# Two layers of linear attention and gated MLP on one core: Strassen for half of K's pairs, a third two-level product in one down stage, and a new order at the start and at the hand-overs

## The chip, the cores and the metric

One Trainium2 chip, one core of it. The metric is the device time of one execution in microseconds; the runs shown are three of the same kernel. A profiled execution gives the trace; its span runs from the first to the last instruction.

Engines in the text: PE (TensorE, matmul), ACT (ScalarE), DVE (VectorE), POOL (GpSimd), SP (SyncE, which issues all DMA here).

## The reference

Sequence 2048, width 1024, 32 heads of 32, MLP width 3584, bf16. The block is applied twice with the same weights:

```python
def _A_ref(x, wqkv, wo):                       # linear attention
    q, k, v = split(x @ wqkv)
    phi = lambda t: where(t > 0, t + 1, exp(t)) + 1e-6
    pq, pk = phi(q), phi(k)
    kv = einsum("bhsd,bhse->bhde", pk, v);  z = einsum("bhsd->bhd", pk)
    o = einsum("bhqd,bhde->bhqe", pq, kv) / (einsum("bhqd,bhd->bhq", pq, z)[..., None] + 1e-6)
    return merge_heads(o) @ wo
def _B_ref(x, w_gate, w_up, w_down):           # gated MLP, no activation
    return ((x @ w_gate) * (x @ w_up)) @ w_down
for _ in range(2):
    x = x + _A_ref(_layernorm(x), A_wqkv, A_wo)
    x = x + _B_ref(_layernorm(x), B_w_gate, B_w_up, B_w_down)
```

## The kernel before

**A program with one order for each engine.** The kernel appends operations to `P.add(engine, ...)` in one hand-chosen order. Each engine runs its own operations in that order; waits are derived from what an operation reads and writes in SBUF pages and PSUM banks, and become semaphores. So the order in which the Python calls are made is the schedule, and an operation late on one engine holds all that is behind it there. All DMAs are issued by SP, in order too. The 16 tiles of 128 rows stay in SBUF (`x_res`); the normalized, transposed input of a stage is `xnT`.

**Layer A** (`layer_A`). In layer one, the projections are plain: `proj_kh` and `proj_qh` do 8 matmuls of 128x512 for one tile and one half of the columns. Layer norm of the next tiles (`LN.start`: statistics; `b_one`: normalize; `step_t`: transpose) is woven between. K goes two tiles ahead of Q (`NHOLD = 2`). For each half, ACT takes the exponential out of PSUM (`ex`) and DVE finishes phi from PSUM and the exponential (`fin`); POOL adds up z (`z_add`). While this goes on, `pt_ops` makes sums of Q's weight blocks (`ptq`, one piece per tile from the fifth) and stores them to `pt_scratch` for layer two.

In layer two, `kq_pairs` does two tiles at a time. K is `plain`: four steps of 8 matmuls a pair. Q is `strassen`: seven steps of 4 matmuls, `st1, st5, st6, st2, st7, st3, st4`, with the transformed weights `T` from `pt_scratch` and sums of the input blocks made by `s_sums`. In a Strassen pair, `st1` and `st5` are followed by ACT copies out of PSUM, and `st6` and `st7` by a DVE `join` that adds a saved product into another bank; the next accumulation into the bank read waits for it. Steps are placed on a line by position (`at(pos, ...)`, with `QLAG`, `QEND`, `LNP`, `SPOS`, `SSTEP`) and run sorted by it: K's and Q's steps alternate, with layer norm steps (`flow_step`) and reloads of the normalized rows (`xr_load`) between. `SEP` says for which of K and Q phi is finished by halves (`fin1`) instead of by whole tiles (`fin2`). K uses PSUM banks 0 to 3, Q 4 to 7, and four buffers hold exponentials (`ebuf`).

Both layers then form `xr^T pk` in chunks (`gchunk`, L1291), multiply by the value weights (`kvt`), normalize queries (`norm`), and multiply by the folded output weights (`y_grp`, 8 matmuls for one tile and one half, L1383). The first steps of the gate/up stage, the list `pro`, can be run early, one PE operation at a time, by `pro_step`.

**Layer B** (`layer_B`). Two passes of 1024 rows. `gateup` works on pairs of column units with Strassen's seven products (L1470), some of them split once more (two-level, L1540). `down` multiplies the hidden activations, held as four blocks `hA` to `hD`, by the down weights, again with seven products, named by digits, in the order `DPROD[ps_]`. A one-level product is 4 row tiles x 14 matmuls of 128x512 (L2020); a two-level one (`two_level`) is 7 steps x 2 x 7 matmuls of 128x256 (L1918), with operand sums from `a_sums`. Weights come through a ring of five slots (`ring_issue`). `d_two` says which products are two-level:

```python
DPROD = ["1274653", "1674253"]

def d_two(first, ps_):
    return "532" if ps_ else "" if first else "53"
```

The second pass (`ps_ = 1`) uses the chained form (`chain_step`): products "1", "6", "7" and "4" accumulate in the same four PSUM banks, DVE takes out each intermediate sum, and the operand for the next product is formed by DVE tile by tile. The first pass uses separate banks and its own sequence. During it, `x_pop` makes the operand sums for the second pass's gate/up, and `stash` and `sp_load` move rows and weight sums.

Layer one's first pass is told apart as `jit`: it makes the gate/up weight sums itself.

**The start.** SP issues row tile 0, K's first weight half, tile 1, K's second half, tile 2, Q's first half, tile 3, Q's second half, and the other tiles. PE starts tile 0 after its normalize and transpose.

Of the kernel before, what the change touches and what calls it, by code (L numbers as in the profile page):

```python
# [180 lines left out]
def build_kernel(nc, A_x, A_wqkv, A_wo, B_w_gate, B_w_up, B_w_down, out):  # L181
    _, S, D = A_x.shape
# [13 lines left out]
    KSTR = False  # L196
    QLAG = 0.284
    QEND = 0.102
    SEP = "q"
    LNP = (0.474, 0.5)  # L200
    SPOS = 0.283
    SSTEP = 0.14
    CUP = 9
    KP0 = 1
# [124 lines left out]
    with ExitStack() as es:  # L329
# [36 lines left out]
        O_RT = [[O_R + i * 2048 for i in range(8)], [RB + SZ_HB + i * 2048 for i in range(9)] + [RE + i * 2048 for i in range(3)]]  # L366
# [93 lines left out]
        def ln_a(i, act=False, oj=0):  # L460
# [9 lines left out]
            for h in range(2):  # L470
                P.add("dve", (lambda h: lambda e: e.bn_stats(st[j][:, 6 * h:6 * h + 6], x_res[:, i, (D // 2) * h:(D // 2) * (h + 1)]))(h),
                      rd=r_x(i, (D // 2) * h, (D // 2) * (h + 1)), wr=R(O_ST[j] + 24 * h, 24))
# [35 lines left out]
        class LN:  # L508
# [26 lines left out]
            def start(self, i):  # L535
                assert i == self.n
                act = self.stat_act
                j = ln_a(self.order[i], act, self.o_junk)
# [174 lines left out]
        DPROD = ["1274653", "1674253"]  # L713

        def d_two(first, ps_):
            return "532" if ps_ else "" if first else "53"

        def d_units(first, ps_):
            r = []
            for q in DPROD[ps_]:  # L720
# [121 lines left out]
        def x_ops(pair, prods, jit=False):  # L842
            t1, t2, t3, t4 = t_ops(pair)
            tp = {q: tp_ops(pair, q, jit) for q in "1325"}
            has = lambda q: [(q, f) for f in tp[q]] if q in prods else []
            return [("t1", t1)] + has("1") + [("t2", t2), ("t3", t3)] + has("3") + [("t4", t4)] + has("2") + has("5")
# [90 lines left out]
        def layer_A(lnp, nxt, first, pro):  # L937
# [11 lines left out]
            def proj(w, rw, i):  # L949
                bank = B_KQ[kq_i[0] % len(B_KQ)]  # L950
                kq_i[0] += 1

                def fn(e):
                    return [e.matmul(psb(bank), xnT[:, k, i * 128:(i + 1) * 128], w[:, k, :],  # L954
                                     start=(k == 0), stop=(k == KT - 1)) for k in range(KT)]
# [12 lines left out]
            def proj_kh(i, h):  # L968
                proj(wkh[first][h], R(O_WKH[first][h], 8192), i)
# [27 lines left out]
            def kq_pairs():  # L997
                BG = {"k": [0, 1, 2, 3], "q": [4, 5, 6, 7]}
                ROLE = [dict(a=0, d=1, b=2, c=3), dict(a=0, b=1, d=2, c=3)]
                OP5 = {"k": RC, "q": RC + 2048 if KSTR else RC + 2 * SZ_SLOT + 4096}  # L1000
# [3 lines left out]
                def at(pos, fn):  # L1004
                    ev.append((pos, len(ev), fn))
# [4 lines left out]
                def bk(kind, p):  # L1010
                    r = ROLE[0 if kind == "k" and (p < KP0 or not KSTR) else p % 2]
# [6 lines left out]

                def ebuf():
                    r = e_cnt[0] % 4  # L1020
                    e_cnt[0] += 1
                    return O_E[r]
# [30 lines left out]
                def plain(kind, p):  # L1053
# [4 lines left out]
                    def step(i, h, bank, last, other):  # L1058
                        if h == 0:
                            eb[i] = ebuf()  # L1060
# [1185 lines left out]
```

## Time and profile before

| | |
|---|---|
| median of three runs | 1447.18 us |
| runs | 1447.4, 1445.64, 1447.18 us |
| profiled execution, its own time | 1446.97 us |
| its span | 1445.2 us |
| granted TensorE clock | full speed |
| HBM read, written | 237.24 MB, 62.13 MB |
| matmuls | 8294 |
| K/Q matmuls of layer two, plain (L945) and Strassen (L1115) | 288 and 196 |
| down matmuls, one-level (L2020) and two-level (L1918) | 1120 and 784 |

The page gives for each engine the busy time, its share of the span and the number of instructions. The chain of work that ended last is followed back from the last instruction; its shares say which engine set the end. In a group's row, the part behind the first bar is busy time and mean duration of one, and the part behind the second is how long the engine stood idle just before these instructions and what released it. In a timeline row, the first figure is the start, the second the length, and the bracket the idle time before it and its releaser. Stages by time in this trace: layer A of layer one to about 243 us, its MLP to 737, layer A of layer two to 960 (K and Q to 836), its MLP to the end.

### The profile page before, as it was taken

The page shows a single profiled execution, that of the slowest core. Times are in us where ns is not written, and L with a number is a line of the kernel's source. Part 1 is how long each engine was busy: PE and PEld are TensorE (multiplying, and loading weights), DVE is VectorE, ACT ScalarE, POOL GpSimd, SP SyncE. Part 2 cuts the span into 40 slices and gives each one's busy share as a digit, 9 for nine tenths or more (in the row PEclk, how much of TensorE's full clock was granted, in tenths as well). Part 3 has the DMA queues.
Part 4 walks back from the last instruction along what each step waited for, and adds up shares of the span by engine and source line. Part 5 has one row for each costly group of instructions (what it writes and reads, how often), then busy time and mean ns, then how long its engine had stood idle before and what let it go on. Part 6 is the DMA issues. An engine that isn't in the chain of part 4 may idle for free.

```text
span 1445.2 us, 21993 instructions
## 1 busy us (share of the span) xinstructions
PE 1433.9 (99%) x8294; PEld 800.4 (55%) x8294; DVE 1128.6 (78%) x2027; ACT 680.2 (47%) x1438; POOL 227.5 (16%) x260
## 2 busy tenths in 40 slices
PE   8999999999999999999999999999999999999999
PEld 3444444555544555554664444456666457666547
DVE  6766889889867799877677779879877786777856
ACT  3652256677720255550156423567777005777401
POOL 4543733000000000000044346300000000000000
PEclk9999999999999999999999999999999999999999
DMA  6334757987879899986896067679975779887657
GB/s 233 88 79 118 151 125 155 290 298 249 294 288 338 262 271 294 293 257 225 253 341 195 0 173 151 155 213 274 282 260 197 241 247 296 264 264 257 205 164 239
DMA packets 377993, 324.41 MB, mean 224 GB/s; under 512 B 178208, under 2 KB 326048, under 8 KB 377632
## 3 DMA queue, kind: packets, MB, share of 16 engines
q1 hardware_dynamic: 377888, 323.02, 74.5%
q8 instruction: 65, 1.06, 0.3%
q14 instruction: 40, 0.33, 0.1%
HBM read 237.24 MB, written 62.13 MB: 207 GB/s over the span
## 4 chain that ended last, share of the span: by engine, by line
PE 92%; DVE 4%; DMA 2%; ACT 1%; issue 0%; SPq 0%; POOL 0%; DVEq 0%
PE ps L1470 25%; PE ps L1540 17%; PE ps L2020 16%; PE ps L1291 8%; PE ps L954 6%; PE ps L1383 6%; PE ps L1918 6%; PE ps L945 4%; PE ps L1115 3%; DVE arena L821 2%; DVE arena L824 1%; DMA arena<-in_A_wqkv_dram 1%; DMA arena<-in_B_w_up_dram 1%; DMA arena<-in_B_w_down_dram 1%; PE ps L1303 0%
## 5 line engine op out<-in xcount | busy, mean ns | idle before, releaser
L821 DVE TENSOR_TENSOR arena<-arena 128x512 f16<-128x512 f16 (+7 forms) x752 | 414.1, 577 | 75.9 <-ACT arena L1584 47.6
L1470 PE MATMUL ps<-arena 128*128 128x512 f16 x1808 | 446.5, 379 | 0.7 <-ACT ps L1500 0.7
L824 DVE SCALAR_TENSOR_TENSOR arena<-ps,arena 128x512 f16<-128x512 f32 (+2 forms) x448 | 298.8, 686 | 76.0 <-PE ps L2020 52.2
L1540 PE MATMUL ps<-arena 128*128 128x256 f16 x2324 | 311.8, 273 | 1.7 <-DVE ps L1559 1.3
L1540 PEld LDWEIGHTS ps<-arena 128*128 128x128 f16 (+1 forms) x2324 | 226.2, 98 | 105.0 <-DVE ps L1559 5.8
L1470 PEld LDWEIGHTS ps<-arena 128*128 128x128 f16 (+1 forms) x1808 | 176.4, 98 | 141.8 <-ACT ps L1500 1.4
L2020 PE MATMUL ps<-arena 128*128 128x512 f16 (+1 forms) x1120 | 243.2, 379 | 0.0
L2020 PEld LDWEIGHTS ps<-arena 128*128 128x128 f16 x1120 | 109.6, 98 | 131.3
L1475 ACT ACTIVATE arena<-ps 128x512 f16<-128x512 f32 x224 | 134.0, 598 | 94.0 <-PE ps L1470 90.8
L1556 ACT COPY ps<-ps 128x256 f32<-128x256 f32 x220 | 81.1, 369 | 128.5 <-PE ps L1540 121.4
L1559 DVE TENSOR_TENSOR ps<-ps,arena 128x256 f32<-128x256 f32 x220 | 92.3, 428 | 36.5 <-PE ps L1540 18.4
L474 POOL TENSOR_SCALAR arena<-arena 128x1 f32<-128x1 f32 x48 | 19.5, 407 | 626.1 <-DVE arena L473 626.1
L954 PE MATMUL ps<-arena 128*128 128x512 bf16 x512 | 112.5, 379 | 3.8 <-DMA arena<-in_A_wqkv_dram 1.1
L1291 PE MATMUL ps<-arena 128*128 128x512 bf16 x512 | 115.4, 379 | 0.0
L1383 PE MATMUL ps<-arena 128*128 128x512 bf16 x512 | 111.0, 379 | 0.0
L1922 ACT COPY ps<-ps 128x256 f32<-128x256 f32 x32 | 11.4, 357 | 209.2 <-PE ps L1918 147.1
L1214 POOL TENSOR_TENSOR arena<-arena 128x1024 f16<-128x1024 f32 x32 | 79.2, 2476 | 70.2 <-DVE arena L1212 69.0
L1500 ACT COPY ps<-ps 128x512 f32<-128x512 f32 x112 | 64.2, 573 | 52.0 <-PE ps L1540 44.5
L1918 PE MATMUL ps<-arena 128*128 128x256 f16 (+1 forms) x784 | 87.0, 273 | 0.1
L978 POOL TENSOR_TENSOR arena<-arena 128x512 f32<-128x512 f32 x60 | 74.8, 1266 | 74.1 <-DVE arena L1040 44.0
L954 PEld LDWEIGHTS ps<-arena 128*128 128x128 f16 x512 | 49.5, 98 | 63.0 <-DMA arena<-in_A_wqkv_dram 1.6
L1383 PEld LDWEIGHTS ps<-arena 128*128 128x128 f16 x512 | 50.1, 98 | 60.2
(77 smaller groups left out, 1215.6 us busy)
## 6 DMA issues: line engine op xcount, KB each, us to landing
arena<-w_scratch SPq DMA_DIRECT2D x84, 512.0 KB, 4.9
arena<-sp_scratch SPq DMA_DIRECT2D x56, 512.0 KB, 5.8
arena<-t_scratch SPq DMA_DIRECT2D x29, 896.0 KB, 6.8
arena<-in_B_w_down_dram SPq DMA_DIRECT2D x21, 896.0 KB, 6.9
w_scratch<-arena SPq DMA_DIRECT2D x28, 512.0 KB, 6.5
sp_scratch<-arena SPq DMA_DIRECT2D x28, 512.0 KB, 4.1
arena<-in_B_w_gate_dram SPq DMA_DIRECT2D x42, 256.0 KB, 5.0
arena<-in_B_w_up_dram SPq DMA_DIRECT2D x42, 256.0 KB, 3.2
```

Source lines behind the costliest of these rows:

```text
L821: P.add("dve", lambda e: e.tensor_tensor(out=out, in0=a, in1=b, op=op), rd=rd, wr=wr, prd=prd)
L824: P.add("dve", lambda e: e.scalar_tensor_tensor(out=out, in0=a, scalar=sc, in1=b, op0=ALU.mult, op1=op1), rd=rd, wr=wr, prd=prd)
L954: return [e.matmul(psb(bank), xnT[:, k, i * 128:(i + 1) * 128], w[:, k, :], start=(k == 0), stop=(k == KT - 1)) for k in range(KT)]
L1291: return [e.matmul(psb(bank), xr[:, t, j * 128:(j + 1) * 128], pk[:, h, t, :], start=(t == 0), stop=(t == NST - 1)) for t in range(NST)]
L1383: return [e.matmul(psb(bank), xnT[:, g, i * 128:(i + 1) * 128], wp[:, g, dh * 512:(dh + 1) * 512], start=(dh == 0 and g == 0), stop=(g == ...
L1470: P.add("pe", lambda e: [e.matmul(psb(bank), w[:, k, :], x[:, k, :], start=(start and k == 0), stop=(k == 3), skip_group_check=True) for k ...
L1475: P.add("act", lambda e: e.activation(t, psb(bank), AF.Copy, scale=SG), prd=[bank], wr=r)
L1540: P.add("pe", lambda e: [e.matmul(psb(bank)[:, 256 * half:256 * half + 256], w[:, k, :], xx[:, k, :], start=(start and k == 0), stop=(k == ...
L1556: P.add("act", lambda e: e.copy(psb(dst[c])[:, 0:256], lo), prd=[bk], pwr=[dst[c]])
L1559: P.add("dve", lambda e: e.tensor_tensor(out=psb(dst[c])[:, 256:512], in0=lo, in1=c5, op=ALU.add), prd=[bk], rd=rc5, pwr=[dst[c]])
L1918: P.add("pe", lambda e: [e.matmul(psb(bank)[:, 256 * half:256 * half + 256], a[:, k, :], w[:, k, :], start=(start and k == 0), stop=(k == ...
L2020: return [e.matmul(psb(bank), hv[:, 7 * hf + k, t * 128:(t + 1) * 128], w[:, k, :], start=(start and hf == 0 and k == 0), stop=(hf == 1 an ...
```

## The change

- **Loads at the start:** tile 1 goes ahead of K's first weight half, and the other tiles come one place earlier against the weights.
- **Start of layer one's layer A:** the first half of tile 1's statistics goes ahead of tile 0's normalize on DVE; tile 1's transpose goes between the two halves of tile 0's first eight matmuls; K's first column half is done for tiles 0 and 1 before the second. The order of K and Q is the same (K first) throughout.
- **Strassen for K:** `KSTR = True`, `KP0 = 4`: K's pairs 4 to 7 of layer two use `strassen`. Layer one makes sums of K's weight blocks too and stores them (`ptq` gets five more pieces), and layer two loads them at its start; Q's first block of the second column half is loaded at the end of the stage.
- **Order of layer two's K/Q stage:** written out in `KQ_SEQ` in place of the sort by position. Phi is finished one step later (`pend`), by halves for K too (`SEP = "qk"`), with three exponential buffers (`NEB = 3`), because the fourth holds a saved product.
- **Early heads:** the first gate step of layer one (`P1A+`) and up to three steps of layer two's prologue run between the last `y` groups.
- **Layer two's first down stage:** the chained order, and product "2" two-level as well as "5" and "3"; the sums for it lie in the used part of `xnT`, and its intermediate sums in other buffers (`O_RT`), one of them row tile 15's, after it is stashed. `x_pop`, `stash` and one `sp_load` move to other products.

```diff
-    KSTR = False
-    QLAG = 0.284
-    QEND = 0.102
-    SEP = "q"
+    KSTR = True
+    NEB = 3
+    KQ_SEQ = "K00 S00 S01 K01 S02 S03 L K02 K03 K10 L X K11 Q00 K12 Q01 X L ... X Q64 L Q65 Q66 V W O"
+    SEP = "qk"
...
-    KP0 = 1
+    KP0 = 4
...
-        DPROD = ["1274653", "1674253"]
+        DPROD = {(True, 0): "1274653", (True, 1): "1674253", (False, 0): "1674253", (False, 1): "1674253"}
+        DTWO = {(True, 0): "", (True, 1): "532", (False, 0): "532", (False, 1): L2D}
...
+                def fin1(*a):
+                    pend.append(lambda: fin1_(*a))
...
-                for _, _, f in sorted(ev, key=lambda t: t[:2]):
+                for _, _, tk, f in run:
+                    if tk[0] not in "KQ":
+                        f()
+                        continue
+                    if tk[2] == "0":
+                        flush()
+                    n = len(pend)
                     f()
+                    for _ in range(min(n, len(pend))):
+                        pend.pop(0)()
+                flush()
...
             if first:
                 lnp.start(0)
-                lnp.b_one()
-                lnp.start(1)
+                lnp.start(1, lnp.b_one)
...
+                proj_kh(0, 0, b0, range(4))
+                lnp.step_t(1)
+                proj_kh(0, 0, b0, range(4, KT))
+                ev[0][0](0)
+                lnp.b_one()
+                lnp.start(3)
+                proj_kh(1, 0, b2)
+                ev[1][0](0)
+                lnp.step_t(1)
+                for i, b in enumerate((b1, b3)):
+                    proj_kh(i, 1, b)
...
+                if not first and i == NST - 1:
+                    pro_step(pro, 1)
                 y_grp(tok[i], 0, i)
...
+                if i == NST - 2 or not first and i == NST - 1:
+                    pro_step(pro, 1)
...
-                npro = 0 if jit else [tk[:2] in early for _, tk in seq].index(False)
+                npro = [tk[:2] in early for _, tk in seq].index(False)
+                if jit:
+                    npro = 1
+                    seq.insert(0, seq.pop([tk for _, tk in seq].index("P1A+")))
...
-                if ps_:
+                chain = ps_ or not first
+                if chain:
                     hs.update({"7": (hE, RB), "3": (hA, O_HA)})
...
-                if q == "2" and t == 3:
+                if q == ("2" if first else "1") and t == 3:
                     for k in range(5):
                         stash(11 + k)
...
+                elif not first and q in "453":
+                    x_pop({"4": 2, "5": 1 if t > 1 else 0, "3": 3}[q])
...
-                if q == "3" and t == 0 and not first:
+                if q == "3" and t == 2 and not first:
                     sp_load(1, 1, "53")
...
+        xload(1)
         load_w("k", 0)
-        xload(1)
+        xload(2)
         load_w("k", 1)
-        xload(2)
+        xload(3)
         load_w("q", 0)
-        xload(3)
+        xload(4)
+        xload(5)
         load_w("q", 1)
```

220 lines of the change are left out of this document (136 added, 84 removed).

## The prediction

> **What bounds the kernel now.** I read the page first: busy times, then the chain, then the groups.
>
> ```profile
> span 1445.2 us, 21993 instructions
> ...
> PE 1433.9 (99%) x8294; PEld 800.4 (55%) x8294; DVE 1128.6 (78%) x2027; ACT 680.2 (47%) x1438; POOL 227.5 (16%) x260
> ...
> PE 92%; DVE 4%; DMA 2%; ACT 1%; issue 0%; SPq 0%; POOL 0%; DVEq 0%
> ```
>
> TensorE is busy 99% of the span and holds 92% of the chain. What one matmul costs is its spacing in an unbroken run, which the chain in order of time gives (start, length, what).
>
> ```profile
> 61.87 55.41 PE ps L954 x256
> ...
> 1361.75 48.35 PE ps L2020 x224
> 1410.10 32.24 PE ps L1918 x294
> ```
>
> A 512-column matmul costs 55.41/256 = 0.2164 us or 48.35/224 = 0.2158 us, a 256-column one 32.24/294 = 0.1097 us. So a matmul that goes is worth its whole spacing, if the other engines still feed PE. Next the waits of PE (engine, line, releaser: us, times, longest):
>
> ```profile
> PE ps L1540 <- DVE ps L1559: 1.3, 2, 0.7
> PE ps L954 <- DMA arena<-in_A_wqkv_dram: 1.1, 1, 1.1
> PE ps L954 <- ACT arena L598: 1.1, 1, 1.1
> ...
> PE ps L954 <- DVE arena L662: 0.5, 1, 0.5
> PE ps L1115 <- DVE ps L1119: 0.2, 1, 0.2
> ```
>
> PE waits little, and most of it at the start and where layer A hands over to layer B. That is all that better ordering can win; the rest must come from matmuls.
>
> **Part 1: matmuls removed.** Layer two's K projection: pairs 4 to 7 of eight go from `plain` (4 steps of 8) to `strassen` (7 steps of 4), so 4 x (32 - 28) = 16 matmuls of 512 columns go: 16 x 0.2164 = 3.46 us. Layer two's first down stage: product "2" goes from 4 tiles x 14 = 56 matmuls of 512 to 7 x 2 x 7 = 98 of 256: 56 x 0.2158 = 12.08 against 98 x 0.1097 = 10.75, so 1.33 us go. Together 4.8 us.
>
> The Trainium skill speaks against the second: "TensorE: Matmul & The Clock Gate", Back-to-back issue gap, gives a sustained 131 ns at 512 columns and 81 ns at 128. Taken straight between, an estimate from that page, 256 columns cost about 98 ns, and the product would grow by about 2.3 us. The trace has 216 and 110 ns over hundreds of matmuls, and the measurement decides.
>
> **Part 2: the start.** The timeline of the first 20 us, and a piece of the chain (eight transposes):
>
> ```profile
> 5.77 0.55 DVE L504 TENSOR_SCALAR arena<-arena 128x1024 f16<-128x1024 bf16 x1 [1.00 <-POOL arena L476]
> ...
> 7.93 1.90 PE L954 MATMUL ps<-arena 128*128 128x512 bf16 x8 [0.94 <-ACT arena L590]
> ...
> 7.98 1.42 DVE L471 BATCH_NORM_STATS2 arena<-arena 128x6 f32<-128x512 bf16 x2 [1.67 <-DMA arena<-in_A_x_dram]
> ...
> 9.44 0.21 DVE L473 BATCH_NORM_AGGREGATE arena<-arena 128x2 f32<-128x12 f32 x1
> ...
> 10.98 1.90 PE L954 MATMUL ps<-arena 128*128 128x512 bf16 x8 [1.15 <-DMA arena<-in_A_wqkv_dram]
> ...
> 11.71 1.42 DVE L471 BATCH_NORM_STATS2 arena<-arena 128x6 f32<-128x512 bf16 x2 [0.51 <-DMA arena<-in_A_x_dram]
> ...
> 13.41 1.01 ACT L598 COPY arena<-ps 128x1024 f16<-128x1024 f16 x1
> ...
> 14.47 3.63 PE L954 MATMUL ps<-arena 128*128 128x512 bf16 x16 [1.15 <-ACT arena L598]
> ...
> 18.10 0.45 PE ps L596 x8
> ```
>
> Eight matmuls take 1.73 us, so PE stands from 9.66 to 10.98 (second half of K's weights) and, after eight more and 0.45 of transposes, from 13.16 to 14.47 (copy of tile 1): 2.63 us. Loads land in the order issued: tile 1 by 7.98, the second weight half by 10.98, tile 2 by 11.71. With tile 1 ahead of the first weight half, that half lands last of the same bytes, at 7.98 (0.05 later than PE starts now). Tile 1 lands some 3 us before that (the 1 MB between 7.98 and 10.98), at about 5. Its first statistics half fits DVE's 1.00 us wait for POOL if it is there by then; otherwise tile 0's normalize behind it slips, by 0.7 (half of 1.42) at most. DVE then has tile 1 normalized at about 8.8: normalize 0 to 6.3, second half 0.7, aggregate 0.2, POOL 1.0, normalize 0.55. PE: four matmuls to 8.85, transposes to 9.3, four more to 10.2; the copy (1.01) ends at about 10.5, so 0.3 is left as wait. Then tile 1's first half, tile 2's transposes, and the second weight half (now with tile 2's old place, 11.71) is needed at 12.7. Query weights have one tile more ahead of them, and queries start one step later. Gain 2.63 - 0.3 - 0.05 = 2.3, lower end 1.5.
>
> **Part 3: the two hand-overs.** Layer one, then layer two:
>
> ```profile
> 242.20 1.03 PE L1470 MATMUL ps<-arena 128*128 128x512 f16 x4
> ...
> 243.89 2.33 PE L1470 MATMUL ps<-arena 128*128 128x512 f16 x10 [0.67 <-ACT ps L1500]
> ...
> 961.76 1.92 PE L1540 MATMUL ps<-arena 128*128 128x256 f16 x14 [0.55 <-DVE ps L1559]
> ...
> 963.06 0.33 PEld L1540 LDWEIGHTS ps<-arena 128*128 128x128 bf16 x4 [0.32 <-DVE ps L1559]
> ...
> 963.82 1.21 PEld L1540 LDWEIGHTS ps<-arena 128*128 128x128 f16 x12 [0.43 <-ACT arena L1584]
> ```
>
> The first four gate matmuls end issuing at 243.06 and the next wait till 243.89 for a copy that stands behind two evictions on ACT: 0.83. `P1A+` now goes ahead of y's last-but-one second half; 24 matmuls of y (5.2 us) cover the copy. I take 0.8; lower end 0, if DVE, late there, gives it back. In layer two three prologue steps instead of one go between y groups of 1.73 us, which covers most of 0.55 + 0.32 + 0.43 = 1.3: I take 0.8.
>
> **Part 4: what the K/Q stage of layer two pays.** Stage 737 to 836 us, without layer norm in its second half; windows there (length, PE, PEld, DVE, ACT, POOL, clock, DMA) and DVE's groups by form:
>
> ```profile
> 789.00:802.00 13.00, 13.00 (x62) 5.88 (x60) 10.00 (x16) 6.01 (x11) 4.53 (x4) 1.00 0.01 2
> 802.00:815.00 13.00, 13.00 (x62) 5.86 (x61) 7.41 (x12) 6.22 (x11) 4.53 (x4) 1.00 0.00 0
> L1050 DVE SCALAR_TENSOR_TENSOR arena<-ps,arena 128x512 bf16<-128x512 f32 x10 | 6.8, 687 | 2.7 <-ACT arena L1027 2.6
> L1040 DVE SCALAR_TENSOR_TENSOR arena<-ps,arena 128x1024 bf16<-128x1024 f32 x4 | 4.9, 1224 | 0.1
> L1119 DVE TENSOR_TENSOR ps<-ps,arena 128x512 f32<-128x512 f32 x4 | 2.8, 690 | 0.0
> L647 DVE TENSOR_SCALAR arena<-arena 128x1024 bf16<-128x1024 bf16 x4 | 1.7, 424 | 1.6 <-ACT arena L1031 1.5
> L645 DVE TENSOR_SCALAR arena<-arena 128x512 bf16<-128x512 bf16 x2 | 0.6, 294 | 4.0 <-ACT arena L1031 4.0
> ```
>
> The 26 us hold two K and two Q pairs; DVE is busy 17.4, 8.7 a pair. A Strassen K pair costs DVE 2 x 0.690 + 4 x (0.687 + 0.294) = 5.30 instead of 2 x (1.224 + 0.424) = 3.30: 10.7 of the 56 x 0.2164 = 12.1 us that PE then takes, 88%. ACT gets two more PSUM copies a pair and stays near 60%. Finishing phi a step later puts the joins, on which PE waits, ahead of it on DVE and takes away waits on ACT such as the 4.0 and 2.6 above. Three exp buffers for four tiles in flight work the other way. Bounds: the 0.2 of the waits of PE won, or 4 us lost (half of the added 2.0 in each of the four pairs, what an engine at 88% that works in order may not find room for). I take 0.6 lost, nearer the row. K's transformed weights are two more 1 MB loads, last in SP's queue as the stage begins; layer norm's stores and transposes stand behind them. Their first use comes after 200 matmuls, 43 us, and the tiles that wait for those transposes are pairs 5 and later: cost nothing, or what the loads lack of those 43 us.
>
> **Part 5: what layer one pays.** Four more weight sums for K, one per step, like Q's (first row), and a 2 MB store (last row):
>
> ```profile
> 57.90 1.80 DVE L821 TENSOR_TENSOR arena<-arena 128x2048 f16<-128x2048 bf16 x1
> 57.47 3.25 POOL L978 TENSOR_TENSOR arena<-arena 128x512 f32<-128x512 f32 x2 [1.72 <-DVE arena L662]
> 790.38 2.27 POOL L978 TENSOR_TENSOR arena<-arena 128x512 f32<-128x512 f32 x2 [4.64 <-DVE arena L1040]
> 88.38 0.55 DVE L497 TENSOR_SCALAR arena<-arena 128x1024 f16<-128x1024 bf16 x1 [2.46 <-POOL arena L487]
> pt_scratch<-arena SPq DMA_DIRECT2D x1, 2048.0 KB, 6.8
> ```
>
> A step has 2.46 us of idle DVE before its normalize, more than 1.80. But z's two adds on POOL take 3.25 beside such a sum and 2.27 without, and POOL's pow behind them holds that normalize. Q's four sums cost PE 0.5 once; K's cost 0 to 1.4, I take 0.4. On SP the store stands ahead of V's and wo's loads, which wait for its 6.8 us in the shared buffer; V is first used only when the projections have ended and two chunks of the kv sum have run: cost nothing.
>
> The Trainium skill, "SBUF — State Buffer", Who interferes with whom, says a DVE instruction with two SBUF inputs and a GpSimd instruction that reads SBUF exclude each other for its whole length. The 3.25 against 2.27 agrees. By it alone up to 4 x 1.0 would be lost, which is rival two.
>
> **Part 6: the down stage around the product.** Chaining "1", "6", "7", "4" adds DVE work per tile: two sums and an eviction in "1".
>
> ```profile
> L821 DVE TENSOR_TENSOR arena<-arena 128x1792 f16<-128x1792 f16 x24 | 25.8, 1083 | 0.1
> L824 DVE SCALAR_TENSOR_TENSOR arena<-ps,arena 128x512 f32<-128x512 f32 x24 | 16.2, 687 | 9.0 <-PE ps L2020 8.9
> ```
>
> 2 x 1.083 + 0.687 = 2.85 of 14 x 0.2158 = 3.02 us a tile fits, as it does in the second stage (48.35 for 224, unbroken). The operand sums for the next gate/up pass move to "4", "5" and "3". In "5" DVE has 4 x 1.083 + 8 x 0.687 = 9.8, four joins and two small sums against PE's 10.75: it ends a little late, and "3", with half the evictions, gives that back. Moved DMAs: the five stashes go one product earlier, the last `sp_load` waits for an eviction two ticks later and holds the ring loads behind it on SP, whose slots are five units ahead. The product also loads 1.4 MB more through that ring. I take 0; ends -0.5 (the size of a PE wait on DVE in the rows of waits) and +1 (a lag of one 1.083 sum that stays).
>
> **Sum.** -4.8 - 2.3 - 0.8 - 0.8 + 0.6 + 0.4 = -7.7. The profiled execution took 1446.97 us, 1.77 more than its span; the median of the runs is 0.21 above it. 1446.97 - 7.7 = 1439.3.
>
> **Rivals.** One more group, of 256-column matmuls in groups of two:
>
> ```profile
> L1540 PE MATMUL ps<-arena 128*128 128x256 f16 x2324 | 311.8, 273 | 1.7 <-DVE ps L1559 1.3
> ```
>
> 1. DVE sets the pace of the K/Q stage's second half. For: 88%, in order. Against: under 90%, and PE waited on a join for only 0.2 there. Costs the upper 4 instead of 0.6, with tails 1441 to 1444.5: 1442.7.
> 2. POOL's z adds held up in layer one: 4 x (3.25 - 2.27) = 3.9 instead of 0.4: 1442.8. Against: Q's four cost 0.5.
> 3. Slower than before: the three exp buffers. ACT's exp must wait for DVE to finish phi two tiles back, ACT's copies queue behind it, PE's next accumulation behind them. Thirty tiles take a buffer; it decides from (7.7 + 2.9)/30 = 0.35 us a tile, about a third of one finish (0.98). At 0.5 a tile, 15 us: 1454. Against: PE's longest wait on DVE there is 0.2 now.
> 4. 256-column matmuls cost more than their columns: at L1540's 311.8/2324 = 0.134 the product takes 13.1 and loses 1.0 instead of winning 1.3: 1441.7. Against: the 0.1097 above. The Trainium skill's issue gap, cited in part 1, points the same way; the trace disagrees with it.
> 5. K's pairs aren't switched (the condition is `p < KP0 or not KSTR`): 3.46 less won: 1442.8.
> 6. Better: waits gone in full, none new: -4.8 - 2.6 - 0.8 - 1.3 - 0.3 = -9.8: 1437.2.
>
> **How the numbers follow.** Forecast 0.60; rivals 0.17, 0.06, 0.05, 0.02, 0.03, 0.07. A difference under 0.2% (2.9 us) can't be told from none by this measurement. Faster by more: all but rival 3 and the upper tail of rival 1 (0.03): 0.92; same 0.03; slower 0.05. Range 1436.8 to 1443.6: it takes in rivals 2, 4, 5, most of 1 and 6, and leaves out 3 and the tails.
>
> **What would show it.** 128 matmuls fewer in the group of L945 and 56 fewer in that of L2020, 112 more in L1115's and 98 more in L1918's; PE busy lower by about 5. PE's waits at L954 for weights and L598 near 0.3 in sum, those at L1470 and L1540 at the hand-overs under 0.5. In the K/Q stage DVE near 80 us and PE waits on L1119 or on ACT's copies under 1. It is wrong if PE's waits there pass 4 us, or if the four extra L821 128x2048 sums leave PE standing in layer one.

## The result, and the profile after

| | before | changed |
|---|---|---|
| median of six runs each | 1447.29 us | 1441.28 us |
| lowest and highest | 1445.64, 1449.32 | 1440.58, 1443.13 |
| ratio, 95% interval | | 0.996 [0.9947, 0.9972] |
| profiled execution: time, span | 1446.97, 1445.2 us | 1440.99, 1439.0 us |

Forecast: 1439.3 us, with a range of 1436.8 to 1443.6. The total came out 2.0 us high, inside the range; one term of the sum did not hold at all. The lines move in the changed file: L954 is L965, L945 is L955, L1115 is L1146, L1470 is L1536, L1540 is L1606, L1918 is L2001, L2020 is L2106, L821 is L828, L824 is L831.

The page of the changed kernel: span, busy time of the engines, and the chain's shares.

```profile
span 1439.0 us, 22106 instructions
...
PE 1430.1 (99%) x8320; PEld 804.0 (56%) x8320; DVE 1143.5 (79%) x2053; ACT 687.4 (48%) x1452; POOL 231.1 (16%) x260
...
PE 97%; DVE 1%; DMA 1%; ACT 0%; SPq 0%; issue 0%; ACTq 0%
```

TensorE has 3.8 us less to do (about 5 had been forecast) and holds 97% of the chain, not 92%. The groups show that the matmuls were moved as counted: 128 fewer in `plain`, 112 more in `strassen`, 98 more of 256 columns, 56 fewer of 512.

```profile
L2106 PE MATMUL ps<-arena 128*128 128x512 f16 (+1 forms) x1064 | 231.1, 379 | 0.0
...
L2001 PE MATMUL ps<-arena 128*128 128x256 f16 (+1 forms) x882 | 98.1, 273 | 0.4 <-DVE ps L2008 0.3
...
L1146 PE MATMUL ps<-arena 128*128 128x512 f16 (+1 forms) x308 | 68.4, 379 | 0.0
...
L955 PE MATMUL ps<-arena 128*128 128x512 bf16 x160 | 37.0, 379 | 0.0
```

All waits of PE that the profile of the changed kernel lists (releaser: us, times, longest):

```profile
PE ps L965 <- DMA arena<-in_A_wqkv_dram: 2.5, 1, 2.5
PE ps L444 <- POOL arena L440: 1.4, 1, 1.4
PE ps L1606 <- ACT arena L1650: 0.6, 2, 0.4
PE ps L594 <- DVE arena L510: 0.6, 1, 0.6
PE ps L1536 <- ACT arena L1541: 0.5, 1, 0.5
PE ps L2001 <- DVE ps L2008: 0.3, 1, 0.3
```

The hand-overs and the K/Q stage wait less than before; the first line is longer than anything in the list before. Two traces of the same program are best compared at stage marks: the start of the first matmul of a stage. The table gives the stage lengths between them in us, and the terms of the sum that belong there.

| stage on PE | before | changed | difference | forecast |
|---|---|---|---|---|
| start and layer one's attention, to the first chunk | 117.12 | 117.33 | +0.21 | -2.3 + 0.4 |
| layer one, first chunk to first down matmul | 291.04 | 290.02 | -1.02 | -0.8 |
| rest of layer one | 328.83 | 328.84 | 0.0 | 0 |
| K/Q stage of layer two | 98.33 | 94.22 | -4.11 | -3.46 + 0.6 |
| layer two, first chunk to first down matmul | 284.77 | 284.25 | -0.52 | -0.8 |
| first down stage and gate/up of pass two | 241.50 | 240.74 | -0.76 | -1.33 |
| last down stage | 80.73 | 80.73 | 0.0 | 0 |
| sum | 1442.32 | 1436.13 | -6.2 | -7.7 |

**The start.** The chain in order of time (start, length, what):

```profile
2.18 7.39 DMA arena<-in_A_wqkv_dram
9.58 0.14 issue
9.71 1.38 PE ps L965 x4
11.10 0.85 PE ps L602 x8
11.95 3.49 PE ps L965 x12
15.44 0.45 PE ps L602 x8
15.89 4.32 PE ps L965 x20
...
778.65 51.91 PE ps L1146 x240
...
1114.82 48.36 PE ps L2106 x224
...
1403.91 32.23 PE ps L2001 x294
```

K's first weight half lands at 9.58, not at 7.98. Behind it eight transposes take 0.85 instead of 0.45, and twelve matmuls 3.49 instead of 2.6. The windows have the reason (length, busy time of PE, PEld, DVE, ACT and POOL, and at the end the clock, the DMA share and GB/s):

```profile
0.00:9.58 9.58, 5.25 (x18) 1.98 (x18) 4.06 (x8) 2.36 (x3) 4.21 (x24) 1.00 0.80 256
10.00:12.00 2.00, 2.00 (x13) 1.28 (x12) 1.60 (x3) 0.01 (x1) 0.00 (x0) 0.56 1.08 359
12.00:14.00 2.00, 2.00 (x7) 0.69 (x6) 0.58 (x2) 1.30 (x2) 0.79 (x2) 0.59 1.11 353
```

The granted clock is 0.56 and 0.59 from 10 to 14 us. Single matmuls start every 0.427 us instead of 0.216 between 10.2 and 13.7 us, after PE had stood idle from 7.20 to 9.71. Added up over the matmuls and transposes of that stretch, this costs 1.67 us.

**The K/Q stage.** The 240 matmuls at 778.65 run unbroken at 51.91/240 = 0.2163 us. DVE's windows in the same 26 us as before:

```profile
789.00:802.00 13.00, 13.00 (x62) 5.85 (x60) 12.07 (x20) 6.70 (x13) 4.58 (x4) 1.00 0.36 125
802.00:815.00 13.00, 13.00 (x62) 5.90 (x61) 11.07 (x21) 7.86 (x16) 4.59 (x4) 1.00 0.01 1
```

(12.07 + 11.07)/26 = 89%, where 88% had been worked out, and PE waits for nothing in it. Over the whole stage DVE is busy 77.91 us of 94.22; near 80 had been forecast.

### The profile page after: what moved, and what is told of

Its sections match the earlier page's. It is cut to its first block, busy times and chain, and to the rows that moved or that the text cites. A ratio compares the mean times of both kernels' runs of the same rounds, so it can differ in the third digit from the quotient of the medians.

```text
span 1439.0 us, 22106 instructions
## 1 busy us (share of the span) xinstructions
PE 1430.1 (99%) x8320; PEld 804.0 (56%) x8320; DVE 1143.5 (79%) x2053; ACT 687.4 (48%) x1452; POOL 231.1 (16%) x260
## 4 chain that ended last, share of the span: by engine, by line
PE 97%; DVE 1%; DMA 1%; ACT 0%; SPq 0%; issue 0%; ACTq 0%
PE ps L1536 27%; PE ps L1606 17%; PE ps L2106 16%; PE ps L965 8%; PE ps L1447 8%; PE ps L1355 8%; PE ps L2001 6%; PE ps L1146 5%; PE ps L955 2%; DVE arena L828 1%; DMA arena<-in_B_w_up_dram 1%; DMA arena<-in_A_wqkv_dram 1%; PE ps L1367 0%; PE ps L1395 0%; DVE arena L831 0%; PE ps L602 0%
## 5 line engine op out<-in xcount | busy, mean ns | idle before, releaser
L828 DVE TENSOR_TENSOR arena<-arena 128x512 f16<-128x512 f16 (+8 forms) x760 | 423.3, 584 | 74.2 <-ACT arena L1650 46.6
L1536 PE MATMUL ps<-arena 128*128 128x512 f16 x1808 | 446.6, 379 | 0.5 <-ACT arena L1541 0.5
L831 DVE SCALAR_TENSOR_TENSOR arena<-ps,arena 128x512 f16<-128x512 f32 (+2 forms) x440 | 293.5, 685 | 73.1 <-PE ps L2106 50.4
L1606 PE MATMUL ps<-arena 128*128 128x256 f16 x2324 | 312.0, 273 | 0.8 <-ACT arena L1650 0.6
L1606 PEld LDWEIGHTS ps<-arena 128*128 128x128 f16 (+1 forms) x2324 | 226.3, 98 | 104.1 <-DVE ps L1625 4.0
L1536 PEld LDWEIGHTS ps<-arena 128*128 128x128 f16 (+1 forms) x1808 | 176.5, 98 | 141.4 <-ACT arena L1541 1.4
L2106 PE MATMUL ps<-arena 128*128 128x512 f16 (+1 forms) x1064 | 231.1, 379 | 0.0
L2106 PEld LDWEIGHTS ps<-arena 128*128 128x128 f16 x1064 | 104.1, 98 | 124.7
L965 PE MATMUL ps<-arena 128*128 128x512 bf16 x512 | 113.4, 382 | 2.5 <-DMA arena<-in_A_wqkv_dram 2.5
L2001 PE MATMUL ps<-arena 128*128 128x256 f16 (+1 forms) x882 | 98.1, 273 | 0.4 <-DVE ps L2008 0.3
L2001 PEld LDWEIGHTS ps<-arena 128*128 128x128 f16 x882 | 85.6, 98 | 12.6 <-DVE ps L2008 1.0
L989 POOL TENSOR_TENSOR arena<-arena 128x512 f32<-128x512 f32 x60 | 78.6, 1330 | 67.5 <-DVE arena L1079 29.6
L965 PEld LDWEIGHTS ps<-arena 128*128 128x128 f16 x512 | 50.1, 98 | 61.7 <-issue 3.6
```

The costliest lines, as they stand in the source:

```text
L828: P.add("dve", lambda e: e.tensor_tensor(out=out, in0=a, in1=b, op=op), rd=rd, wr=wr, prd=prd)
L831: P.add("dve", lambda e: e.scalar_tensor_tensor(out=out, in0=a, scalar=sc, in1=b, op0=ALU.mult, op1=op1), rd=rd, wr=wr, prd=prd)
L1536: P.add("pe", lambda e: [e.matmul(psb(bank), w[:, k, :], x[:, k, :], start=(start and k == 0), stop=(k == 3), skip_group_check=True) for k ...
L1606: P.add("pe", lambda e: [e.matmul(psb(bank)[:, 256 * half:256 * half + 256], w[:, k, :], xx[:, k, :], start=(start and k == 0), stop=(k == ...
L2001: P.add("pe", lambda e: [e.matmul(psb(bank)[:, 256 * half:256 * half + 256], a[:, k, :], w[:, k, :], start=(start and k == 0), stop=(k == ...
L2106: return [e.matmul(psb(bank), hv[:, 7 * hf + k, t * 128:(t + 1) * 128], w[:, k, :], start=(start and hf == 0 and k == 0), stop=(hf == 1 an ...
```

## The experiments

The table has, for each kernel, when K's first weight half lands (two numbers where it comes in two pieces), whether PE ran at half clock in its first projections, the first chunk's mark, the length from there to the first down matmul of layer one, and the time.

| kernel | weights land | half clock | first chunk | to first down | time, us (runs) |
|---|---|---|---|---|---|
| before | 7.26 | no | 117.12 | 291.04 | 1447.29 (6) |
| changed | 9.58 | yes | 117.33 | 290.02 | 1441.28 (6) |
| e1 | 6.92 | yes | 117.81 | 291.51 | 1443.03 (8) |
| e2 | 8.49 | no | 115.66 | 294.72 | 1441.43 (6) |
| e3 | 5.47, 7.70 | no | 115.03 | 291.96 | 1440.71 (5) |
| e4 | 8.03 | yes | 115.78 | 291.64 | 1444.53 (1) |
| e5 | 8.65 | yes | 117.06 | 290.78 | 1442.32 (1) |
| e6 | 8.75 | yes | 116.49 | 291.76 | 1443.64 (1) |
| e7 | 8.52 | yes | 116.26 | 290.28 | 1439.92 (1) |
| e8 | 5.69, 7.86 | no | 115.20 | 290.40 | 1439.42 (1) |
| e9 | 8.23 | yes | 115.97 | 290.89 | 1439.42 (5) |
| e10 | 6.31, 8.45 | yes | 117.09 | 290.37 | 1439.39 (5) |
| e11 | 5.84, 8.01 | no | 115.32 | 289.17 | 1438.94 (5) |
| e12 | 7.64 | yes | 118.46 | 289.38 | 1441.10 (5) |

The marks are those of one profiled execution, the time is the median of the runs. Ratios are to runs of the kernel before on the same chip, whose medians were 1447.30 (e1 to e4), 1446.13 (e5 to e8, one run), 1447.29 (e9 to e11) and 1447.02 (e12). The profiled executions of e9 and e10 were the slowest of their five (1441.29 and 1441.60), that of e2 the second slowest of six (1444.12): marks are read for the mechanism, medians for the gain. The length to the first down matmul differs from one execution to the next: with the changed kernel's start and loads of w_down it is 290.02, 291.64, 290.78, 291.76 and 290.28 (changed, e4 to e7).

### e1: the loads and first statistics of before, with the new order on PE

```diff
-        xload(1)
         load_w("k", 0)
-        xload(2)
+        xload(1)
         load_w("k", 1)
-        xload(3)
+        xload(2)
 ...
-                lnp.start(1, lnp.b_one)
+                lnp.b_one()
+                lnp.start(1)
```

> The changed kernel with the start's loads and the first statistics in the order of before; PE's new order at the start is kept. Theory one (the load order costs): K's first weight half lands near 7.3 us as before, PE's first projection begins near 7.9 us instead of 9.7 and runs at full clock; tile 1's copy ends near 12.9, the first four K groups end near 18.5 instead of 19.2; the kv chunks begin near 116.8 instead of 117.5 and the total is about 0.7 us less, 1440.6. Theory two (PE's new order of the first groups costs by itself): the chunks begin no earlier than 117.5 and the total stays at 1441.3.

Measured: 1443.03 us, ratio 0.9971 [0.9961, 0.9981]. The weights land at 6.92, but then the tile that PE wants next is late, the clock is at half for two stretches of 3.4 us, and the first chunk comes at 117.81. With the order that PE now has, the old loads and statistics are 1.75 us worse by the medians (some runs overlap: the lowest is 1440.61). Theory one had 0.7 us less and is wrong: the new order of the loads is not what lost the start.

### e2: twelve matmuls of zeros behind tile 0's transposes

```diff
+                P.add("pe", lambda e: [e.matmul(psb(B_KVT[1]), wrm[:, 0:128], wrm, start=True, stop=True)
+                                       for _ in range(12)], ...)
```

> The changed kernel with twelve 512-column matmuls on zeros right behind tile 0's transposes (2.6 us at full clock, into a bank not in use), which fill the time that PE waits for weights. If half of the loss at the start is the lower TensorE clock after that idle time (spacing 427 ns instead of 216 between 10.1 and 13.8 us), the first groups run at full clock, the chunks begin near 116.2 instead of 117.5 and the total falls by about 1.3 us to 1440.0. If the late weights alone cost, nothing moves: 117.5 and 1441.3.

Measured: the clock stays whole and the first chunk comes at 115.66, 1.7 us sooner than in the changed kernel. Of this, 0.42 is its first projection, at 9.29 instead of 9.71; the rest comes with the full clock. But the median is 1441.43, where 1440.0 had been expected. In the profiled execution, one of its slow ones, the chain in layer one's first gate/up pairs shows where the gain went:

```profile
270.32 8.54 DMA arena<-in_B_w_down_dram
...
278.88 0.70 DVE arena L828
...
281.51 0.60 DVE arena L831
...
283.17 0.35 DVE ps L1627
...
283.57 0.83 PE ps L1608 x6
```

DVE has the sums for the transformed down weights (`wd_prep`, L828) at the head of its queue when their load is still on its way, from 270.32 to 278.86. Behind them stand the eviction (L831) and the join (L1627) for which PE waits, 2.75 us. After that idle time the clock falls once more, at 284.88 (windows of e2, clock third from the end):

```profile
280.00:284.00 4.00, 1.25 (x8) 0.60 (x7) 3.96 (x9) 1.47 (x3) 0.00 (x0) 1.00 1.15 322
284.00:288.00 4.00, 4.00 (x16) 1.80 (x15) 3.90 (x10) 1.78 (x4) 0.00 (x0) 0.61 0.83 281
```

### e3: K's first weight half in two pieces, tile 1 between them

```diff
+        wk_half(0)
         xload(1)
-        load_w("k", 0)
+        wk_half(1)
         xload(2)
```

(`wk_half(r)` loads four of the eight blocks of 128 rows, 512 KB; the first statistics are in the order of before.)

> The changed kernel with K's first weight half loaded as two pieces of 512 KB (rows 0 to 3 and 4 to 7 of the contraction), tile 1 between them, and the statistics in the order of before. Theory one: the first piece lands before 7 us, PE starts near 7.9 us at full clock, tile 1 is normalized near 9.7 instead of 11.3 with the old order, the first four groups end near 17, the chunks begin near 115.5, the total is 1439.2. Rival: what lands last is set by the slowest of the 16 DMA engines and not by the bytes ahead; then the second piece lands after 9.6, PE waits for it as now, and the chunks begin at 117 or later.

Measured: the pieces land at 5.47 and 7.70, the clock stays whole, the first chunk comes at 115.03, 2.3 us before the changed kernel's: the rival, a second piece after 9.6, is out. At the first down matmul 0.36 us of that are left, and the median is 1440.71, where 1439.2 had been expected. The same stage takes it back: 291.96 instead of 290.02.

### e4: all of K's pairs plain

```diff
-    KP0 = 4
+    KP0 = 8
```

(and `KQ_SEQ` with the four plain steps for pairs 4 to 7)

> The changed kernel with all eight K pairs of layer two plain, four steps a pair at the places of every other Strassen step; K's weight sums are still made, stored and loaded. If Strassen for K is worth its matmuls and nothing else, the stage from the first K matmul to the first chunk grows from 94.2 us by 16 x 0.216 = 3.5 to 97.7 and PE waits stay under 0.3. If Strassen steps cost PE waits of their own, it grows by less; if the order of the stage without them has waits as before (0.7), by up to 4.1 to 98.3.

Measured: the K/Q stage takes 97.76 us instead of 94.22, that is 3.54 for 16 matmuls, where 16 x 0.2164 = 3.46 had been forecast. Part 1 holds for K. The same matmuls took 98.33 before the change, so the new order alone is worth the other 0.57.

### e5: no early heads

```diff
-                if not first and i == NST - 1:
-                    pro_step(pro, 1)
 ...
-                if i == NST - 2 or not first and i == NST - 1:
+                if i == NST - 1:
                     pro_step(pro, 1)
```

(and the longer prologues undone)

> The changed kernel with the heads of both MLPs issued where the kernel before issues them (the early pro_step calls and the longer prologues undone, all else kept). Theory: the early heads are what removed the waits at the two hand-overs. From the first y matmul to the first down matmul of layer one 220.20 -> 221.0 (before 221.22), from y to down of layer two 214.36 -> 214.95 (before 214.95); the end about 1.4 us later. Rival: the hand-overs gained from the earlier x stores and seeds, or the won time turned into later waits of the first pairs: each difference under 0.3 us.

Measured: from the first y matmul to the first down matmul 220.96 us in layer one (changed 220.20, before 221.22) and 214.95 in layer two (214.36, 214.95). Its PE waits between 185 and 290 us have the old one back:

```profile
PE ps L1534 <- ACT ps L1564: 0.7, 1, 0.7
```

In layer two the early heads are worth 0.59 us, and the other traces with them have 214.30 to 214.57 there. In layer one the difference of 0.76 is less than the spread of that stretch with the heads kept (220.20 to 221.94 in the changed kernel, e4, e6 and e7); what shows the gain is the wait of 0.7, which is there before the change and in e5, and in no trace with the heads. Part 3, with 0.8 and 0.8, was near.

### e6: phi finished in its own step

```diff
                 def fin1(*a):
-                    pend.append(lambda: fin1_(*a))
+                    fin1_(*a)
```

(the same for `fin2`)

> The changed kernel with phi of a projected tile finished in its own step, as before the change, not one step later; all else kept. Theory (the prediction's step 4): finishing late puts the joins ahead of phi on DVE, and without it TensorE waits again: K/Q stage of layer two from 94.22 to 94.9 or more (0.65 is the wait that the kernel before had there), at most 98. Rival: the place of phi is worth nothing and DVE's 88% is enough either way: 94.2 +- 0.2.

Measured: the K/Q stage takes 96.25 us, 2.03 more. PE's only wait in it:

```profile
PE ps L1146 <- DVE ps L1150: 1.5, 2, 1.1
```

At 89% DVE is enough only if its joins go first: 1.5 of the 2.03 us stand in this row. The late phi is worth half of the 4.11 us that the stage won.

### e7: the sums for pass two spread otherwise over the down stage

```diff
-                elif not first and q in "453":
-                    x_pop({"4": 2, "5": 1 if t > 1 else 0, "3": 3}[q])
+                elif not first and q in "423":
+                    x_pop({"4": 2, "2": 4 if t == 3 else 0, "3": 2}[q])
```

> The changed kernel with the twelve DVE combinations of x for pass two of layer two spread otherwise over the first down stage (two a tile with product 4, four behind the last tile of product 2, two a tile with product 3). Theory: the 1.8 us of waits between 1167 and 1199 us (0.43 at 1189.5, 0.33 at 1198.7) come of DVE's queue at product 5 and 3, where these combinations stand ahead of the evictions: down stage with hand-over 240.74 -> 240.2 to 240.5. Rival: the waits come of ACT's seeds and the two-level products' own joins: 240.74 +- 0.1.

Measured: 240.47 us for the down stage and gate/up of pass two (240.74 in the changed kernel, 240.75 to 240.76 in e1 to e6). The same comes in e10 to e12, which have this edit too (240.46 to 240.48). So 0.27 of the missing 0.57 was the place of these sums. Before the change PE had no listed wait in this stage; e7 has one left:

```profile
PE ps L1606 <- ACT arena L1650: 0.4, 1, 0.4
```

It is about as large as the rest, 0.3, but what would take it away was not tried.

### e8: e3, and the loads of w_down one tick earlier

```diff
                     if u % 4 == 2:
                         wd_prep(j)
+                    elif u % 4 == 3:
+                        if j + 1 < NJ // 2:
+                            wd_load(j + 1)
                     elif u % 4 == 0:
                         if j:
                             wd_store(j - 1)
-                        if j < NJ // 2:
-                            wd_load(j)
+                        else:
+                            wd_load(0)
```

> The kernel of e3 (K's first weights in two pieces) with each load of w_down for the transformed blocks of layer one issued one tick, about 5.8 us, earlier (right behind the sums of the block before). Theory: the start's gain is given back in layer one's first gate/up pairs because DVE stands at the head of its queue for the landing of that load (269.0 -> 277.2 in e3) and TensorE's product waits behind it, 1.4 us at 280.2: that wait goes, from the first chunk to the first down matmul 291.96 -> 290.5 or less, the end 1.4 us earlier than in e3 (span about 1437.4). Rival: the rings are what is full there (every landing takes 7 to 9 us), and the earlier load only delays the gate and up loads beside it: 291.96 +- 0.4.

Measured: span 1437.4 us, 290.40 from the first chunk to the first down matmul. PE's wait near 280 us, 1.3 in e3, is gone. Of the 1.94 us that e3 gave back in this stage, 1.56 are won back: the wait on that load was most of it. Two waits are left, one of 0.4 that ends at 256.58 and one of 0.6 that ends at 261.21.

### e9: the same on the changed kernel, with its own start

> The changed kernel (start as it is) with the loads of w_down for layer one's transformed blocks one tick earlier, as in e8. Theory: the rings and DVE pace the first gate/up pairs from about 255 us on, and the wait at 280 us appears only where TensorE comes to it early; with the slower start the earlier load takes away little: from the first chunk to the first down matmul 290.0 +- 0.4, and the median within 0.6 of the changed kernel's 1441.28. Rival: the earlier load is worth its 1.4 us by itself: 1439.9.

Measured: 1439.42 us, ratio 0.9945 [0.9931, 0.9958]. That is 1.9 us below the changed kernel; the rival (1439.9) was nearer than the theory, which had at most 0.6. The profiled execution of the changed kernel, from which the theory had its "little", was one in which the weights came late (9.58) and PE reached the pairs after the load. In the others with the same start they land at 8.03 to 8.75; there the wait near 280 us is 1.1 in e4, 1.4 in e6 and 0.2 in e5, and e7 has none. So it comes in some executions and not in others. The edit is the cause of the gain, for it is the only one; where it is won can't be read from this trace, which is that of the slowest run (290.89, no wait near 280, but 0.8 and 0.6 before it).

### e10: e8 and e7 together

> K's first weights in two pieces (e3), w_down a tick earlier (e8) and the combinations of x spread otherwise (e7), together on the changed kernel. Theory: the three are in different stages and add up: 1441.28 - 0.6 (e3) - 1.3 (e8 over e3) - 0.3 (e7) = 1439.1, between 1438.5 and 1439.6. Rival: the start still varies from execution to execution and layer one's pairs level it out: 1440.0 or more.

Measured: 1439.39 us, ratio 0.9948 [0.9936, 0.9961], inside the theory's bounds but no better than e9 without the split of the weights. Its profiled execution had the half clock although the weights came in two pieces. What the split and the moved sums add to e9 is not shown.

### e11: e10, and the first load of w_down in the y loop

```diff
                 if first and i == 9:
                     prep_s(0)
+                    wd_load(0)
 ...
-                if first:
-                    wd_tick(0)
-                else:
+                if not first:
```

> e10 with the first of those loads of w_down issued in the y loop, at its tenth tile (about 217 us), not behind the stores of x at 244.6. Theory: the megabyte is then out of the rings when the loads and stores of the first pairs need them: the load of up weights that DVE waits for (250.0 -> 258.8 in e8) lands about 3 us sooner and the TensorE waits of 0.5 and 0.7 at 255.8 and 260.4 go, about 1 us less than e10: 1438.1. Rival: that load is held up by the weight-sum stores and transposes that are issued with it, and lands within 1 us of where it did: as e10.

Measured: 1438.94 us, ratio 0.9941 [0.9929, 0.9954]. In the changed kernel the chain of that stage is this:

```profile
251.86 0.50 PE ps L1536 x3
252.35 8.22 DMA arena<-in_B_w_up_dram
...
260.60 0.30 DVE arena L828
...
262.31 0.61 ACT arena L1541
...
262.96 1.90 PE ps L1536 x8
```

The load of up weights takes 8.22 us, DVE's sums wait for it, and PE behind them. In e11 the load is issued at 248.78 and landed at 254.11, and the chain there is nothing but PE, for example:

```profile
249.84 1.73 PE ps L1539 x8
251.57 0.44 PE ps L1609 x4
252.00 0.86 PE ps L1539 x4
252.87 0.87 PE ps L1609 x8
```

From the first chunk to the first down matmul it takes 289.17 us with no wait left. This is the fastest version: its slowest run (1439.24) is below the fastest of the changed kernel (1440.58). Against e10 it is 0.45 us by the medians, with runs that overlap, where about 1 had been expected.

### e12: e11 with the loads of before at the start

> e11 with the loads of the start in the order of the kernel before (K's weights ahead of the tiles of x, each half in one piece), nothing else changed. In e11's profile the wait of layer one's first pairs was gone (first chunk to first down matmul 289.17, no wait). Theory: with that wait gone the start is no longer levelled out, so the old loads cost what the stage marks of e1 and e3 say, 117.8 - 115.0 = 2.8 us, less the spread of single executions: the first chunk near 117.5, 289.2 +- 0.3 from it to the first down matmul, median 1440.5 to 1442. Rival: the order of the loads is worth nothing in itself, the clock and the landing vary from one execution to the next: median within 0.7 of e11's 1438.94.

Measured: 1441.10 us, ratio 0.9953 [0.994, 0.9967], 2.2 above e11. Its longest PE wait is at the start:

```profile
PE ps L602 <- DVE arena L510: 2.8, 1, 2.8
```

The first chunk comes at 118.46, and 289.38 to the first down matmul shows that nothing levels it out. So the theory held: once layer one's pairs have no wait on DMA, most of what the start wins is won at the end. Of 3.14 us between the two traces at the first chunk, 2.6 are left in their spans; K/Q of layer two takes 0.54 more in e11, 0.4 of it a wait on its weights.

## Why the forecast held, and which step failed

**Part 1, matmuls removed.** Right: 3.54 for K (e4) against 3.46. For product "2" the spacings held (1114.82: 48.36/224 = 0.2159), but the stage gave 0.76 of 1.33. The upper end of part 6, "a lag of one 1.083 sum that stays", was the right direction: 0.27 of the missing 0.57 is the place of the pass-two sums (e7), the rest is about as large as the one wait that e7 has left.

**Part 2, the start.** Wrong: +0.80 us up to the 33rd projection matmul (18.38 to 19.18) instead of -2.3. The step that failed is "that half lands last of the same bytes, at 7.98". By 9.58 the rings (the queues of the DMA engines) had moved 256 GB/s x 9.58 us = 2.45 MB, but only 1.57 MB stood up to and with that half: the later transfers were well under way when it completed. In the seven profiled executions with these loads (changed, e2, e4 to e7, e9) it landed at 8.03 to 9.58. So 7.98 was an optimist's bound, and the profiled execution of the changed kernel is the latest of the seven; why it is later than the others is open. The other forecasts of this step came true in it: tile 1 landed at 4.53 (about 5) and was normalized at 8.74 (about 8.8). The Trainium skill, "DMA: Bandwidth & Descriptors", Queues, rings and completion order, says that one transfer is split over the rings of up to 16 engines and that completion is not first-in, first-out per issuing engine. No run here shows a landing out of order at the start (the next tile landed at 10.26); what the row shows is that bytes issued behind a load move before it is complete, and a landing time taken from the bytes ahead is then a lower bound.

The second thing that the step left out is the clock: 1.67 us. PE ran at half clock in each of the six executions with this start and nothing for PE to do while it waits, not with e2's zeros. (In e5 it didn't fall, for it had not risen: before 13.55 its matmuls are 0.427 us apart from the first on and its transposes 0.107, not 0.216 and 0.056.) What decided was the idle time in sum, not one long wait. In the 3.41 us ahead of each recorded fall inside the span PE stood idle for 1.98 us or more in all: 2.51 in the changed kernel, 2.08 to 2.47 in e4, e6, e7 and e9, 1.98 in e1, 1.99 in e10, 2.78 in e12, 2.10 ahead of the one of e2 at 284.88. Stretches of that length at full clock that no fall followed have at most 1.15 in the kernel before, 1.21 in e3 and 1.58 in e12. (No single wait in e1's stretch is over 1.08, and the kernel before kept its clock through one of 1.15.) The Trainium skill, "TensorE: Matmul & The Clock Gate", Part 1, has the clock halved after an idle window of about 3.4 us and whole again after as long a busy one, in free-running windows of 3413 ns. The half stretch of 3.41 us, from 10.23 to 13.65, agrees with the length; that the window must be idle throughout does not agree with these sums, and the measurement decides. Sum of the step as it went in the profiled execution: -2.3 + 1.73 (first matmul at 9.71) + 1.67 = +1.1, and 0.3 back, since no wait for tile 1's copy came.

Third, even a better start is worth little at the end as the kernel stands, which no part of the prediction saw: layer one's first gate/up pairs wait for DMA (e2, e3), and a PE that comes earlier can wait longer. The wait was in the prediction's own list. Of the two in its first row, counted there with the start and the hand-overs, one is inside these pairs, at 283.25 us; this is the row of the kernel before from 245 to 290 us:

```profile
PE ps L1540 <- DVE ps L1559: 0.7, 1, 0.7
```

Loads that come earlier (e8, e9, e11) are worth about as much as the start itself, and then the order and the two pieces of the first loads show 2.2 us (e11 against e12).

**Part 3, hand-overs.** Right: the wait of 0.7 in layer one is gone and comes back in e5, and in layer two 0.59 are won (e5), against 0.8 and 0.8. In layer two a wait of 0.4 on ACT (L1650) is left.

**Part 4, the K/Q stage.** Too cautious by 1.2: instead of 0.6 lost, 0.65 more than the matmuls was won, which also lies outside the bounds of that part (0.2 won to 4 lost). The order alone gives 0.57 of it (e4), though the list of PE's waits before has only 0.2 there. The argument was right in its mechanism (e6: without the late phi 2.03 are lost), and the value was taken from the wrong side of zero. Rivals 1 and 3 needed waits that the stage does not have; rival 4 falls with the spacing that the 256-column matmuls kept (1403.91: 32.23/294 = 0.1096; in the changed stage itself 273 of them take 30.82 from 1163.01 on, 0.1129 with a wait in it), rival 5 with the counts, and rival 6 with the start.

**Part 5, layer one's weight sums.** 0 instead of 0.4: from the 33rd projection matmul to the first chunk 98.15 us instead of 98.74. The old wait of 0.5 of L954 on DVE's L662 is gone from the list although four sums were added, so rival 2 is false.

**The sum.** The start's miss (2.1 with part 5) and the down stage's (0.6) add 2.7, the second hand-over 0.3; the K/Q stage and the first hand-over give 1.5 back: -7.7 + 1.5 = -6.2, which is the difference of the spans. That the total lies only 2.0 us from the forecast is in part luck: its range carried the cases, but misses of opposite sign met, 3.0 one way and 1.5 the other.

## What to carry to other kernels

Ask of a gain at the start whether the next stage that is paced by transfers will take it back: find the stage where an in-order engine stands at a load, and compare its marks, of more than one execution, not its share of busy time. A load's landing worked out from the bytes ahead of it is a lower bound, and the idle time that it leaves on TensorE can cost as much again through the clock. On an engine at nearly 90%, put what PE waits for ahead of what nobody waits for; that, not the load, decided here.

## What the runs showed of the hardware

- Of 1 MB issued at 2.18 us, with 0.5 MB ahead and transfers behind, the landing was between 8.03 and 9.58 us in seven profiled executions with the same order of loads; as two transfers of 512 KB, issued at 1.71 and 2.73, it was there at 7.70 to 8.45 in four (e3, e8, e10, e11).
- The granted clock was at half for 3.41 us at a time (6.83 in e1) after stretches of 3.41 us in which TensorE had stood idle for 1.98 to 2.78 us in sum, at the start and again in the middle (e2, from 284.88); stretches with up to 1.58 us of idle time passed without it.
- A load of 512 KB took 8.2 us from issue to landing with a load of 1 MB issued 5.7 us before it (changed kernel, 252.35); with that load moved away, 5.3 (e11, 248.78).
- TensorE waits for weights at the beginning of layer two's K/Q stage in e9, and by 0.4, 0.2 and 0.2 in e11, e10 and e2, but not in the changed kernel's trace. That it comes there earlier does not explain it: e8, which is there at 734.44, has no such wait, and e2, at 739.21, has. The row of e9:

```profile
PE ps L955 <- DMA arena<-in_A_wqkv_dram: 0.5, 1, 0.5
```
